# Sparse attention and a feed-forward layer on one core: key, query and output transposes of the later batches moved from TensorE to DMA

## The chip, the core and the metric

The kernel runs on one core of a Trainium2 chip. The core has five engines that run side by side, each through its own instructions in order: TensorE (PE; its weight loads are listed apart as PEld), VectorE (DVE), ScalarE (ACT), GpSimd (POOL) and SyncE (SP). Transfers run on 16 DMA engines and are issued from the queues of GpSimd and SP. The metric is the device time of one execution in microseconds; lower is better. The time before is 329.82 us, the median of three runs (329.7 to 330.48).

## The reference

Inputs q, k, v have 8 batches, 8 heads, 576 tokens and 64 columns, in float32. The first four heads attend to a band of 32 tokens, the last four to every 32nd token, and the result, laid side by side as 4608 tokens by 512 columns, goes through a feed-forward layer with 2048 hidden columns:

```python
scores = scale * np.matmul(q, k.transpose(0, 1, 3, 2))
rel = pos[:, None] - pos[None, :]
mask_local = (rel >= 0) & (rel < 32)
mask_strided = (rel >= 0) & (pos[None, :] % 32 == pos[:, None] % 32)
...                                     # heads 0-3 band, heads 4-7 strided
attn = softmax(np.where(mask, scores, -1e9))
x = np.matmul(attn, v)                  # then (batch, token) x (head, column)
h = x @ w_in
r = np.maximum(h, 0.0)
out = (s * (r * r) + b) @ w_out
```

## The kernel before

**Layouts.** Attention runs by batch `b` (0 to 7) and by pair of heads `m` (0 to 3). Pairs 0 and 1 are band heads ("loc", names ending in `l`), pairs 2 and 3 strided heads ("str", names ending in `s`); `mm` is the pair's number within its kind. For band pairs the 576 tokens lie as 6 pieces of 96; for strided pairs as 8 pieces of 72, each holding the tokens of one residue modulo 8. Scores need queries and keys with the 64 columns on the partitions, so both must be transposed, two heads at a time (128 rows). `qD_loc` and `qD_str` hold the queries of one pair, `kT_loc` its band keys, `kTs` its strided keys. The output of a pair, `x_nat`, has tokens on the partitions and must be transposed once more into `xT[m]`, which the feed-forward layer reads as its moving operand.

**Who transposes.** TensorE does most of it: line 357 for queries and keys (six matmuls against the identity for a band pair, eight for a strided one) and line 529 for outputs. Each result lies in PSUM and is copied out by ACT or DVE (line 286). Band queries and keys first go through a pairing copy (`qp`, `kp`, posted by `pair_post`), which lays two heads side by side. Two kinds go by DMA transpose from SP already: the strided keys from b = 3 on (`k_dma`, line 399) and the band outputs from b = 2 on (`x_dma`, line 551).

**The rest of attention.** Line 429 is the scores, line 443 the exponential on ACT, line 451 the mask on DVE, line 481 the product with v (AV), lines 496 and 507 the division on DVE.

**Feed-forward.** Nine tiles `T` of 512 tokens. Line 574 is the first product (64 matmuls of 512 columns for a tile), line 592 the ReLU on ACT, line 598 the square on DVE, line 609 the second product (again 64), line 620 the eviction on DVE and line 624 the store. A tile needs `xT` of all four pairs for the one or two batches that its tokens belong to.

**What sets the order.** No hardware decides it. A planner written in the kernel, `Plan`, walks through an estimated time and writes one fixed list of instructions for each engine. A `Step` is one TensorE instruction with its estimated ns, the keys it needs and those it makes; `plan.post` places work on the cheapest of the engines it may run on ("A", "V", "P", "D" for ACT, DVE, GpSimd and DMA by SP), when its needs are met in estimated time. A DMA posted as "D" counts 1000 ns and then 5000 ns of latency. Loads get an estimated arrival from `landing(cost)`. In the main loop an attention step is taken while attention is behind `due()`, which grows with the feed-forward steps done, and otherwise a feed-forward step; attention steps come from a window of four pairs. Once the lists stand, an engine waits at each instruction for its real inputs, and nothing behind that instruction can pass it.

**Loads.** `fetch_qk(b)` and `fetch_v(b)` issue a batch's loads from GpSimd, converting float32 to float16 on the way. `ql`, `kl`, `qs` have two buffers each; `ks` are two fixed tiles. From b = 3 on, a fetch is preceded by two tiny copies on GpSimd (line 664), which wait until the strided keys of the batch before have been transposed. The band keys `kl` have 96 partitions, each holding six consecutive tokens of each head (1536 bytes of float32 in one piece). The last load of a batch is its v.

Of the kernel before, what the change touches and what calls it, by code (L numbers as in the profile page):

```python
# [9 lines left out]
FP16 = mybir.dt.float16  # L10
# [100 lines left out]
def kernel(  # L111
# [11 lines left out]
    nc = tc.nc  # L123
    B, H, S, D = q.shape
# [11 lines left out]
    LQ, LT, LPAD = 96, 6, 32  # L136
    SQ, ST = 72, 8
# [16 lines left out]
    inp = ctx.enter_context(tc.tile_pool(name="inp", bufs=2))  # L154
# [26 lines left out]
    kT_loc = [const.tile([128, LPAD + S], FP16, name=f"kT_loc{i}") for i in range(2)]  # L181

    qD_loc = [const.tile([128, LT, 2, LQ], FP16, name=f"qD_loc{i}") for i in range(2)]
    qD_str = [const.tile([128, ST, 2, SQ], FP16, name=f"qD_str{i}") for i in range(2)]
    xT = [const.tile([128, NTOK], FP16, name=f"xT{i}") for i in range(4)]

    SR = 80
    ks = [const.tile([SR, 4 * ST * D], FP16, name=f"ks{i}") for i in range(2)]

    sched = ctx.enter_context(tc.manual_schedule())  # L190
    plan = Plan()

# [3 lines left out]
    NL, NS = 4 * LT * D, 4 * ST * D  # L196
# [3 lines left out]
    def view_l(src, b):  # L200
        return src[b, 0:4].rearrange("h (p j) d -> p h (j d)", j=LT)
# [11 lines left out]
    def h4(ap):  # L213
        return ap.rearrange("p (h x) -> p h x", h=4)
# [21 lines left out]
    loaded = {}  # L236
    paired = {}

    def load_qk(b):
        for name, src in (("q", q), ("k", k)):  # L240
            tl = inp.tile([LQ, NL], FP16, tag=name + "l", name=name + "l")
            nc.gpsimd.dma_start(out=h4(tl), in_=view_l(src, b))
            loaded[b, name + "l"] = tl
        for name, src in (("q", q), ("k", k)):
            ts = inp.tile([SQ, NS], FP16, tag="qs", name="qs") if name == "q" else ks[b % 2]
            if name == "k" and b in (2, 3):
                nc.gpsimd.memset(ts[64:SR], 0.0)
            load_s(ts, src, b)
            loaded[b, name + "s"] = ts

    def load_s(dst, src, b):
        for r in (slice(0, 64), slice(64, SQ)) if b < 2 else (slice(0, SQ),):
            nc.gpsimd.dma_start(out=h4(dst)[r], in_=view_s(src, b)[r])
# [31 lines left out]
    def copy_on(eng, **kw):  # L285
        {"A": nc.scalar.copy, "V": nc.vector.tensor_copy, "P": nc.gpsimd.tensor_copy}[eng](**kw)  # L286

    def pair_post(b, name, mm, key):

        if (b, name) not in paired:  # L290
            paired[b, name] = None

        def g(eng):
            if paired[b, name] is None:
                paired[b, name] = inp.tile([LQ, 2, LT, 2 * D], FP16, tag=name + "p",
                                           name=name + "p")
            from_ = loaded[b, name + "l"]
            copy_on(eng, out=paired[b, name][:, mm].rearrange("p j (e d) -> p e j d", e=2),
                    in_=from_.rearrange("p (m e j d) -> p m e j d", m=2, e=2, d=D)[:, mm])
        plan.post([key], {"A": 810, "V": 350, **({"P": 750.0} if b == 0 else {})}, g,  # L300
                  [("in", name + "l", b, mm)])
# [37 lines left out]
    def pair_steps(b, m):  # L339

        loc = m < 2
        nq, nt = (LQ, LT) if loc else (SQ, ST)
        sfx = "l" if loc else "s"
        mm = m % 2
        nk = 128 if loc else SQ
        st = {}
        steps = []
        id_ = (b, m)
# [43 lines left out]
                    s.posts = [([key], {"A": 640, "V": 757 if loc else 453}, g, [("k", id_), group])]  # L392
            return s

        k_by_dma, x_by_dma = b >= 3, b >= 2

        def k_dma(eng):
            st["k"] = qkp.tile([128, ST, SR], FP16, tag="kTs", name="kTs")
            nc.sync.dma_start_transpose(out=st["k"], in_=ks[b % 2][:, 1024 * mm:1024 * mm + 1024])
            loaded[b, "kTs", mm] = st["k"]  # L400

        if k_by_dma and not loc:

            plan.post([("in", "ks", b, mm), ("s", (b - 1, m), 2)], {"D": 1000.0}, k_dma,
                      [("k", id_)])
        for name in ("q", "k"):
            if k_by_dma and not loc and name == "k":
                continue
            gr = group_of("t", b, m, True)
            for j in range(nt):  # L410
                steps.append(trans(name, j, gr))
        last_t = steps[-1]

        per_s = 2 if loc else 3

# [55 lines left out]
        per = nt if loc else nt // 2  # L471
# [53 lines left out]
        def xtrans(j, group):  # L525
# [21 lines left out]
                s.posts = [([key], {"A": 640, "V": 455 if loc else 756}, g, [("xT", b, m), group])]  # L547
            return s

        def x_dma(eng):  # L550
            nc.sync.dma_start_transpose(
                out=xT[m][:, b * S:(b + 1) * S].rearrange("d (t p) -> d t p", t=nt),
                in_=st["x"].rearrange("p t d -> p (t d)"))

        if x_by_dma and loc:
            plan.post([("x", id_, e, nt - 1) for e in range(2)], {"D": 1000.0}, x_dma,
                      [("xT", b, m)])
        else:
            gr = group_of("t", b, m)
            for j in range(nt):  # L560
                steps.append(xtrans(j, gr))
        return steps, st["last_av"], last_t


    gts = {}
# [77 lines left out]
    def arrive(keys, at):  # L643
        for k in keys:
            plan.done[k] = at
# [4 lines left out]
    def landing(cost):  # L650

        nonlocal ring
        ring = max(ring, plan.t + 2000.0) + cost

        return ring + (6000.0 if plan.t > 60000.0 else 0.0)

    def both(name, b):
        return [("in", name, b, mm) for mm in range(2)]

    def fetch_qk(b):  # L660
        for mm in range(2):
            if (b - 1, "kTs", mm) in loaded:

                nc.gpsimd.tensor_copy(out=gate[0:1, 2 + mm:3 + mm],
                                      in_=loaded[b - 1, "kTs", mm][0:1, 0, 0:1])
        load_qk(b)
        for name in ("q", "k"):
            plan.done["raw", name, b] = landing(1700)
            for mm in range(2):
                pair_post(b, name, mm, ("raw", name, b))  # L670
        for name in ("qs", "ks"):
            arrive(both(name, b), landing(2000))

    def fetch_v(b):
        load_vl(b)
        arrive(both("vl", b), landing(5000))
        if b < LONG_V:
            early_v(b)
        else:
            load_vs(b)  # L680
            arrive(both("vs", b), landing(5000))
# [70 lines left out]
    def when_all(what, b, fn):  # L752

        def g():
            left[what, b] = left.get((what, b), 4) - 1
            if left[what, b] == 0:
                fn()
        return g

    for b in range(B):  # L760
        for m in range(4):
            steps, last_av, last_t = pair_steps(b, m)
            att.append(steps)
            if b + 2 < B:

                last_t.after = when_all("t", b, lambda b=b: plan.post(
                    [("fetch_v", b + 1) if b else ("free",)] +
                    [("k", (bk, mk)) for bk in (b, b + 1 if b > 1 else b) for mk in range(2, 4)],
                    {"P": 0.0},
                    lambda eng: fetch_qk(b + 2), [("fetch", b + 2)]))  # L770
                last_av.after = when_all("av", b, lambda b=b: plan.post(
                    [("fetch", b + 2)] + both("vs", b), {"P": 0.0}, lambda eng: fetch_v(b + 2),
                    [("fetch_v", b + 2)]))
# [55 lines left out]
    while i2 < len(f2) or any(at_i[p] < len(att[p]) for p in range(len(att))):  # L829
# [21 lines left out]
        for o in order:  # L851
            s = f1[i1] if o == 1 else f2[i2]
# [4 lines left out]
        if cand is not None and (att_done < due() or main is None):  # L857
            s = att[cand][at_i[cand]]
# [45 lines left out]
```

The softmax here doesn't subtract the row's maximum and nothing guards it: scores larger than these inputs give would overflow.

## Time and profile before

| | before |
|---|---|
| time, median of 3 | 329.82 us |
| span of the profiled execution | 328.6 us |
| HBM read and written | 38.15 MB, 9.44 MB |
| packets of the GpSimd queue | 50032, 18.65 MB |
| packets of the SP queue | 23114, 13.74 MB |
| PE first product, line 574 | 576 matmuls, of which 432 read the later weight tiles |
| PE second product, line 609 | 576 matmuls |
| PE transposes, lines 357 and 529 | 368 and 152 |
| DMA transposes of xT and kTs | 12 and 10 |

The page gives busy time by engine, then groups of instructions by line, engine and tile. A matmul's duration there overlaps the next one's, so durations of TensorE don't add up to time; distances between starts do. The kernel has three stretches: up to about 40 us inputs and weights arrive and the first attention batch runs; up to about 231 us attention and feed-forward matmuls are mixed; after that only the feed-forward layer is left. The same stretches can be seen in the busy tenths of the 40 slices of the span:

```profile
PE   8898899999999999999999999999999999999995
DVE  5566946698877768676878777586442423332311
ACT  2775943598958856647555556543432433243100
POOL 6482548640931820551065000000000000000000
DMA  7999999999994995599369940131001000101021
```

Each digit is a tenth of the busy share of a slice of 8.2 us. TensorE is full from the sixth slice on, GpSimd, which only issues loads and helps a little at first, ends at about 187 us with the last batch's loads, and the DMA engines show gaps from about 107 us on.

### The profile page before, as it was taken

The page shows a single profiled execution, that of the slowest core. Times are in us where ns is not written, and L with a number is a line of the kernel's source. Part 1 is how long each engine was busy: PE and PEld are TensorE (multiplying, and loading weights), DVE is VectorE, ACT ScalarE, POOL GpSimd, SP SyncE. Part 2 cuts the span into 40 slices and gives each one's busy share as a digit, 9 for nine tenths or more (in the row PEclk, how much of TensorE's full clock was granted, in tenths as well). Part 3 has the DMA queues.
Part 4 walks back from the last instruction along what each step waited for, and adds up shares of the span by engine and source line. Part 5 has one row for each costly group of instructions (what it writes and reads, how often), then busy time and mean ns, then how long its engine had stood idle before and what let it go on. Part 6 is the DMA issues. An engine that isn't in the chain of part 4 may idle for free.

```text
span 328.6 us, 6386 instructions
## 1 busy us (share of the span) xinstructions
PE 318.7 (97%) x2424; PEld 181.7 (55%) x2424; DVE 201.2 (61%) x552; ACT 171.6 (52%) x322; POOL 84.8 (26%) x123
## 2 busy tenths in 40 slices
PE   8898899999999999999999999999999999999995
PEld 3673655666556656556655655555544544444442
DVE  5566946698877768676878777586442423332311
ACT  2775943598958856647555556543432433243100
POOL 6482548640931820551065000000000000000000
PEclk9999999999999999999999999999999999999998
DMA  7999999999994995599369940131001000101021
GB/s 115 184 153 206 214 164 166 219 179 93 141 137 92 163 98 73 66 193 121 72 98 160 81 118 2 50 53 64 2 32 62 36 32 33 64 15 51 32 98 64
DMA packets 73176, 32.80 MB, mean 100 GB/s; under 512 B 54586, under 2 KB 67514, under 8 KB 73146
## 3 DMA queue, kind: packets, MB, share of 16 engines
q0 software_dynamic: 50032, 18.65, 61.1%
q1 hardware_dynamic: 23114, 13.74, 18.3%
q8 instruction: 19, 0.31, 0.4%
q14 instruction: 11, 0.09, 0.1%
HBM read 38.15 MB, written 9.44 MB: 145 GB/s over the span
## 4 chain that ended last, share of the span: by engine, by line
PE 85%; DMA 7%; ACT 4%; POOL 2%; issue 1%; DVE 0%; SPq 0%; POOLq 0%
PE ps_f L609 37%; PE ps_f L574 34%; DMA ql<-in_q_dram 5%; PE ps_s L429 4%; PE ps_a L481 4%; PE ps_t L357 3%; DMA w_out_sb<-in_v_dram 2%; PE ps_t L529 1%; PE ps_a L632 1%; ACT pt L443 1%; ACT qD_str L286 1%; ACT qD_loc L286 1%; POOL w_in L273 1%; POOL v_loc L286 1%; ACT xT L286 0%
## 5 line engine op out<-in xcount | busy, mean ns | idle before, releaser
L609 PE MATMUL ps_f<-w_out_sb,gT 128*128 128x512 f16 x576 | 151.6, 379 | 0.3 <-DVE gT L598 0.3
L592 ACT ACTIVATE u<-ps_f 128x512 f16<-128x512 f32 x136 | 80.6, 596 | 81.7 <-PE ps_f L574 61.1
L574 PE MATMUL ps_f<-xT,w_in_sb 128*128 128x512 f16 x432 | 118.3, 379 | 1.3 <-DMA w_in_sb<-in_moe_w_in_dram 1.3
L598 DVE TENSOR_TENSOR gT<-u 128x512 f16<-128x512 f16 x144 | 59.7, 419 | 54.2 <-ACT u L592 53.0
L609 PEld LDWEIGHTS <-gT 128*128 128x128 f16 x576 | 54.3, 98 | 49.5 <-DVE gT L598 0.6
L574 PEld LDWEIGHTS <-w_in_sb 128*128 128x128 f16 x432 | 46.5, 114 | 33.3 <-DMA w_in_sb<-in_moe_w_in_dram 2.0
L443 ACT ACTIVATE pt<-ps_s 128x384 f16<-128x384 f32 (+2 forms) x96 | 44.6, 488 | 17.0 <-PE ps_s L429 16.2
L481 PEld LDWEIGHTS <-pt 72*72 72x72 f16 (+1 forms) x448 | 36.9, 119 | 13.9 <-DVE pt L451 0.2
L620 DVE SCALAR_TENSOR_TENSOR o<-ps_f,s_sb,bcs 128x512 f32<-128x512 f32 x36 | 26.8, 746 | 19.7 <-PE ps_f L609 19.5
L574 PE MATMUL ps_f<-xT,w_in 128*128 128x512 f16 x136 | 36.0, 380 | 0.1
L507 DVE TENSOR_TENSOR x_nat<-ps_a,rec 72x256 f16<-72x256 f32 (+1 forms) x76 | 35.0, 461 | 1.6
L260 POOL DMA_DIRECT2D v_loc<-in_v_dram x28 | 24.3, 893 | 1.2 <-issue 0.6
L496 DVE RECIPROCAL rec<-ps_a 72x4 f32<-72x4 f32 (+1 forms) x76 | 13.7, 180 | 17.9 <-PE ps_a L481 15.3
L481 PE MATMUL ps_a<-v_str,pt 72*72 72x65 f16 x204 | 22.8, 196 | 0.0
L574 PEld LDWEIGHTS <-w_in 128*128 128x128 f16 x144 | 15.1, 113 | 9.6
L429 PE MATMUL ps_s<-qD_str,kTs 128*72 128x144 f16 x128 | 18.8, 226 | 0.2 <-ACT kTs L286 0.2
L429 PE MATMUL ps_s<-qD_loc,kT_loc 128*128 128x192 f16 x96 | 17.3, 246 | 0.7 <-ACT pt L443 0.3
L265 POOL DMA_DIRECT2D v_str<-in_v_dram x16 | 13.6, 849 | 13.7 <-PE ps_f L574 2.7
L481 PE MATMUL ps_a<-v_loc,pt 128*96 128x65 f16 x150 | 17.1, 203 | 0.0
L451 DVE TENSOR_TENSOR pt<-pt,mask_loc 128x384 f16<-128x384 f16 x42 | 14.4, 351 | 3.9 <-ACT pt L443 3.6
L451 DVE TENSOR_TENSOR pt<-pt,mask_str 72x432 f16<-72x432 f16 (+1 forms) x42 | 14.1, 348 | 3.6 <-ACT pt L443 3.3
L429 PEld LDWEIGHTS <-kTs 128*72 128x72 f16 x128 | 12.7, 113 | 5.4 <-issue 0.7
(91 smaller groups left out, 283.6 us busy)
## 6 DMA issues: line engine op xcount, KB each, us to landing
out_dram<-o SPq DMA_DIRECT2D x36, 256.0 KB, 2.0
ql<-in_q_dram POOLq DMA_DIRECT2D x8, 288.0 KB, 5.2
kl<-in_k_dram POOLq DMA_DIRECT2D x8, 288.0 KB, 6.5
v_loc<-in_v_dram POOLq DMA_DIRECT2D x28, 80.0 KB, 9.3
w_out_sb<-in_moe_w_out_dram POOLq DMA_DIRECT2D x4, 512.0 KB, 12.0
qs<-in_q_dram POOLq DMA_DIRECT2D x6, 288.0 KB, 8.0
ks<-in_k_dram POOLq DMA_DIRECT2D x6, 288.0 KB, 9.2
v_str<-in_v_dram POOLq DMA_DIRECT2D x16, 72.0 KB, 7.0
```

Source lines behind the costliest of these rows:

```text
L260: nc.gpsimd.dma_start(out=vl[:, h, 1:LT, 0:D], in_=rest[:, h])
L429: nc.tensor.matmul(out=st["s", g][0:nk, c:c + 2 * nq], lhsT=(st["k"][:, i * nq:i * nq + nk] if loc else st["k"][:, i, 0:SQ]), rhs=st["q"][ ...
L443: nc.scalar.activation(out=pt[0:nk, 0:2 * n].rearrange("k t c -> k (t c)"), in_=st["s", g][0:nk, 0:2 * n * nq], func=AF.Exp, scale=scale)
L451: nc.vector.tensor_tensor(out=pt[0:nk, 0:2 * n], in0=pt[0:nk, 0:2 * n], in1=mask, op=ALU.mult)
L481: nc.tensor.matmul(out=st["a"][0:nq, j % per, :], lhsT=st["pt", g][0:nk, i, :], rhs=vt[0:nk, 2 * mm + e, j, :])
L496: nc.vector.reciprocal(out=st["rec", e, j][0:nq, 0:per], in_=st["pa", e, j][0:nq, 0:per, D:D + 1])
L507: nc.vector.tensor_tensor(out=st["x"][:, j0:j0 + per, 64 * e:64 * e + 64], in0=st["pa", e, j][0:nq, 0:per, 0:D], in1=st["rec", e, j][0:nq, ...
L574: nc.tensor.matmul(out=gts["h", T, ft], lhsT=(w_in_sb[min(ft // 4, 2) - 1][:, ct, :] if ft > 3 else w_in0[ct]).rearrange("p (c x l) -> p c ...
L592: nc.scalar.activation(out=gts["u", T, ft], in_=gts["h", T, ft], func=AF.Relu)
L598: nc.vector.tensor_tensor(out=gts[T][:, ft, :], in0=u, in1=u, op=ALU.mult)
L609: nc.tensor.matmul(out=gts["o", T, ts], lhsT=gts[T][:, ft, ts * 128:(ts + 1) * 128], rhs=w_out_sb[:, ft, :], start=(ft == 0), stop=(ft == ...
L620: nc.vector.scalar_tensor_tensor(out=o, in0=gts["o", T, ts], scalar=s_sb[:, 0:1], in1=bcs, op0=ALU.mult, op1=ALU.add)
```

## The change

From b = 3 on, three more kinds of transpose leave TensorE. The band keys are loaded in another layout (token 96 t + p on partition p), so that no pairing copy is needed, and `kT_loc` is written by a DMA transpose straight from `kl`. The strided queries are transposed by DMA into a tile `qTs` in SBUF, and a copy (`q_spread`) spreads that over `qD_str`. The strided outputs can't be put into token order by the transpose itself, so `x_out` stores them to a buffer in DRAM in token order and `x_in` transposes them from there into `xT`. TensorE keeps the band queries, the scores and AV, and all transposes of the first three batches. [...] `qs` becomes a tile of 80 rows whose last 16 are cleared once. The fetch of batch b + 2 is now posted once per batch, with the queries and keys of batch b among its needs. The purpose is to take work from TensorE.

```diff
+    KB_DMA, QS_DMA, XS_DMA = 3, 3, 3
+    x_dram = [tc.dram_tile([S, 128], FP16, name=f"x_dram{i}") for i in range(4)]
...
+            if name == "k" and b >= KB_DMA:
+                dst = tl.rearrange("p (m t e d) -> p m e t d", m=2, t=LT, e=2)
+                for h in range(4):
+                    nc.gpsimd.dma_start(out=dst[:, h // 2, h % 2],
+                                        in_=src[b, h].rearrange("(t p) d -> p t d", p=LQ))
+            else:
+                nc.gpsimd.dma_start(out=h4(tl), in_=view_l(src, b))
...
-        k_by_dma, x_by_dma = b >= 3, b >= 2
+        k_by_dma = b >= (KB_DMA if loc else 3)
+        q_by_dma = b >= QS_DMA and not loc
+        x_by_dma = b >= (2 if loc else XS_DMA)
         def k_dma(eng):
+            if loc:
+                st["k"] = kT_loc[mm]
+                nc.sync.dma_start_transpose(
+                    out=st["k"][:, LPAD:LPAD + S].rearrange("d (t p) -> d t p", t=nt),
+                    in_=loaded[b, "kl"][:, 768 * mm:768 * mm + 768])
+                return
...
+        def q_dma(eng):
+            st["qT"] = inp.tile([128, ST, SR], FP16, tag="kp", name="qTs")
+            nc.sync.dma_start_transpose(out=st["qT"],
+                                        in_=loaded[b, "qs"][:, 1024 * mm:1024 * mm + 1024])
+        def q_spread(eng):
+            st["q"] = qD_str[mm]
+            for e in range(2):
+                hs = slice(64 * e, 64 * e + 64)
+                copy_on(eng, out=st["q"][hs, :, e, :], in_=st["qT"][hs, :, 0:SQ])
...
+            plan.post([("in", "qs", b, mm), ("s", (b - 1, m), 2)], {"D": 1000.0}, q_dma,
+                      [("qT", id_)])
+            plan.post([("qT", id_)], {"P": 2000.0, "V": 560.0, "A": 1300.0}, q_spread,
+                      [("q", id_)])
...
+        def x_out(eng):
+            nc.sync.dma_start(out=x_dram[2 * (b % 2) + mm].rearrange("(p j) d -> p j d", j=nt),
+                              in_=st["x"])
+        def x_in(eng):
+            nc.sync.dma_start_transpose(out=xT[m][:, b * S:(b + 1) * S],
+                                        in_=x_dram[2 * (b % 2) + mm])
...
+            plan.post([("x", id_, e, j) for e in range(2) for j in (per - 1, nt - 1)],
+                      {"D": 1000.0}, x_out, [("xd", id_)])
+            plan.post([("xd", id_)], {"D": 1000.0}, x_in, [("xT", b, m)])
...
+            if name == "k" and b >= KB_DMA:
+                arrive(both("kl", b), landing(4600))
+                continue
...
-                last_t.after = when_all("t", b, lambda b=b: plan.post(
-                    [("fetch_v", b + 1) if b else ("free",)] +
-                    [("k", (bk, mk)) for bk in (b, b + 1 if b > 1 else b) for mk in range(2, 4)],
-                    {"P": 0.0},
-                    lambda eng: fetch_qk(b + 2), [("fetch", b + 2)]))
+                if m == 0:
+                    plan.post(
+                        [("fetch_v", b + 1) if b else ("free",)] +
+                        [("q", (b, mk)) for mk in range(4)] + [("k", (b, mk)) for mk in range(4)] +
+                        [("k", (b + 1 if b > 1 else b, mk)) for mk in range(2, 4)],
+                        {"P": 0.0}, lambda eng, b=b: fetch_qk(b + 2), [("fetch", b + 2)])
```

More of the change, by code (lines that the diff above doesn't have):

```diff
@@ L241, in load_qk @@
             tl = inp.tile([LQ, NL], FP16, tag=name + "l", name=name + "l")
-            nc.gpsimd.dma_start(out=h4(tl), in_=view_l(src, b))
             loaded[b, name + "l"] = tl
-        for name, src in (("q", q), ("k", k)):
-            ts = inp.tile([SQ, NS], FP16, tag="qs", name="qs") if name == "q" else ks[b % 2]
-            if name == "k" and b in (2, 3):
+            if name == "k" and b >= KB_DMA:
[5 more added lines that the diff above has]
+                nc.gpsimd.dma_start(out=h4(tl), in_=view_l(src, b))
+        for name, src in (("q", q), ("k", k)):
+            if name == "k":
+                ts = ks[b % 2]
+            elif b < QS_DMA + 2:
+                ts = inp.tile([SR, NS], FP16, tag="qs", name="qs")
+            else:
+                ts = loaded[b - 2, "qs"]
+            if name == "k" and b in (2, 3) or name == "q" and b in (QS_DMA, QS_DMA + 1):
                 nc.gpsimd.memset(ts[64:SR], 0.0)
@@ L294, in g @@
             if paired[b, name] is None:
-                paired[b, name] = inp.tile([LQ, 2, LT, 2 * D], FP16, tag=name + "p",
-                                           name=name + "p")
+                paired[b, name] = inp.tile([128, 2, LT, 2 * D], FP16, tag=name + "p",
+                                           name=name + "p")[0:LQ]
             from_ = loaded[b, name + "l"]
@@ L400, in k_dma @@
             loaded[b, "kTs", mm] = st["k"]
-        if k_by_dma and not loc:
-            plan.post([("in", "ks", b, mm), ("s", (b - 1, m), 2)], {"D": 1000.0}, k_dma,
-                      [("k", id_)])
+        def q_dma(eng):
[7 more added lines that the diff above has]
+                copy_on(eng, out=st["q"][hs, :, e, :], in_=st["qT"][hs, :, 0:SQ])
+        if k_by_dma:
+            plan.post([("in", "k" + sfx, b, mm), ("s", (b - 1, m), 2)], {"D": 1000.0}, k_dma,
+                      [("k", id_)])
+        if q_by_dma:
+            plan.post([("in", "qs", b, mm), ("s", (b - 1, m), 2)], {"D": 1000.0}, q_dma,
+                      [("qT", id_)])
+            plan.post([("qT", id_)], {"P": 2000.0, "V": 560.0, "A": 1300.0}, q_spread,
+                      [("q", id_)])
         for name in ("q", "k"):
-            if k_by_dma and not loc and name == "k":
+            if (k_by_dma if name == "k" else q_by_dma):
                 continue
@@ L411, in pair_steps @@
                 steps.append(trans(name, j, gr))
-        last_t = steps[-1]
         per_s = 2 if loc else 3
@@ L557, in pair_steps @@
                       [("xT", b, m)])
+        elif x_by_dma:
+            plan.post([("x", id_, e, j) for e in range(2) for j in (per - 1, nt - 1)],
+                      {"D": 1000.0}, x_out, [("xd", id_)])
+            plan.post([("xd", id_)], {"D": 1000.0}, x_in, [("xT", b, m)])
         else:
@@ L561, in pair_steps @@
                 steps.append(xtrans(j, gr))
-        return steps, st["last_av"], last_t
+        return steps, st["last_av"]
     gts = {}
@@ L761 @@
         for m in range(4):
-            steps, last_av, last_t = pair_steps(b, m)
+            steps, last_av = pair_steps(b, m)
             att.append(steps)
             if b + 2 < B:
-                last_t.after = when_all("t", b, lambda b=b: plan.post(
-                    [("fetch_v", b + 1) if b else ("free",)] +
-                    [("k", (bk, mk)) for bk in (b, b + 1 if b > 1 else b) for mk in range(2, 4)],
-                    {"P": 0.0},
-                    lambda eng: fetch_qk(b + 2), [("fetch", b + 2)]))
+                if m == 0:
[4 more added lines that the diff above has]
+                        {"P": 0.0}, lambda eng, b=b: fetch_qk(b + 2), [("fetch", b + 2)])
                 last_av.after = when_all("av", b, lambda b=b: plan.post(
```

## The prediction

> **What bounds the kernel now.** I read the busy times first, then the chain that ended last, then TensorE's timeline, and only then the waits and the transfers.
>
> ```profile
> PE 318.7 (97%) x2424; PEld 181.7 (55%) x2424; DVE 201.2 (61%) x552; ACT 171.6 (52%) x322; POOL 84.8 (26%) x123
> ...
> PE 85%; DMA 7%; ACT 4%; POOL 2%; issue 1%; DVE 0%; SPq 0%; POOLq 0%
> ```
>
> The first line is the busy row of the page, the second the chain by engine. PE is busy 97% of the span and is 85% of the chain; the DMA and ACT shares lie in the start-up, before about 40 us. PE overlaps its matmuls, so the busy share does not say what one instruction costs. The timeline does, by the distance from one start to the next (columns: start, busy, engine, line, operation, tiles, count):
>
> ```profile
> 208.18 0.29 PE L357 MATMUL ps_t<-ident,kp 96*128 96x96 f16 x3
> 208.31 0.38 PE L574 MATMUL ps_f<-xT,w_in_sb 128*128 128x512 f16 x1
> ...
> 230.70 0.29 PE L529 MATMUL ps_t<-ident,x_nat 72*128 72x72 f16 x4
> 230.83 1.03 PE L574 MATMUL ps_f<-xT,w_in 128*128 128x512 f16 x4
> 231.70 0.30 PE L529 MATMUL ps_t<-ident,x_nat 72*128 72x72 f16 x4
> ```
>
> Three band-key transposes move the next start by 0.13 us (43 ns each), four strided transposes by 0.13 us (33 ns each), four 512-column matmuls by 0.87 us (216 ns each). From 72 us to the last matmul at 324.4 us, those spacings times the instruction counts leave only 1.2 us over, nearly all at 89.9-91.3 us. So after 72 us the time is the sum of TensorE's spacings: what leaves TensorE leaves the end, and every new wait of TensorE is added to it.
>
> The next views are a line of the waits (total, times, longest), and the landings of one transpose:
>
> ```profile
> POOL gate L664 <- DMA kTs<-ks: 52.0, 8, 11.5
> ```
>
> ```profile
> L551 SPq DMA_TRANSPOSE xT<-x_nat x12: 1197/1217/1302, 70.4 to 217.4; - x12
> ...
> DMA to landing us min/median/max: 2.5/2.6/7.7
> ```
>
> Last, busy time by stage (PE, PE loads, DVE, ACT, POOL, then clock, DMA share, GB/s):
>
> ```profile
> 57.00:81.00 24.00, 23.76 (x245) 15.24 (x244) 18.98 (x60) 18.69 (x36) 9.63 (x12) 1.00 1.36 166
> 81.00:105.00 24.00, 23.64 (x219) 14.62 (x218) 19.69 (x61) 18.00 (x36) 11.13 (x15) 1.00 1.49 128
> 105.00:135.00 30.00, 30.00 (x253) 18.06 (x252) 22.02 (x65) 20.44 (x40) 10.55 (x15) 1.00 1.28 106
> ```
>
> GpSimd waits 52 us in eight waits for the strided keys' transposes before it fetches: loads have slack. A DMA transpose holds SP for 1.2 us and lands in 2.6 us, but the one issued at 70.4 us, among loads, took 7.7. DVE and ACT have 20-30% to spare per stage.
>
> **What the skill says.** "TensorE: Matmul & The Clock Gate", Part 4: PE-mode transpose, gives about 275 ns for a transpose inside a kernel; at that price 220 would be 60 us. This trace has 196-206 ns of duration and 33-43 ns of spacing; the measurement decides. "DMA: Bandwidth & Descriptors", Specifications, puts full rate at pieces of 512 B or more; the packet records agree: 128 B take 32 ns, 768 B 79 ns. The same page, Issuing engines are not separate DMA queues, says that all queues share 16 engines; the 2.5 against 7.7 us above agrees. The same page, Two DMAs through the same engine are not ordered, has a reader of DMA-written bytes wait for the first DMA's semaphore; hence the wait between the two halves of the trip through DRAM. The trace of before has no such pair.
>
> **The change, part by part** (batches count from b = 0; it acts on b = 3 to 7).
>
> TensorE loses 10 band-key pairs x 6 = 60 at 43 ns = 2.6 us, 10 strided-query pairs x 8 = 80 at 33-35 ns = 2.7 us, 10 strided-output pairs x 8 = 80 at 33 ns = 2.6 us. Sum **7.9 us, all on the path**; nothing is added there. With no new wait: 329.8 - 7.9 = 321.9.
>
> ACT and DVE lose 10 band-key evictions, 10 output evictions (the xT copy from PSUM is 0.64 us on ACT) and the key pairing copies (kp, 0.35 us on DVE). The query evictions become copies from SBUF of the same size (6 pairs on DVE, 3 on ACT, 1 on GpSimd). Worth nothing: both engines were off the path.
>
> The planner paces attention by TensorE time, so cheaper batches come sooner: by the order of instructions the last AV matmul is followed by 502 of the 1152 feed-forward matmuls instead of 434, and a batch of attention takes some 26 us instead of 30. Costs nothing while loads keep up.
>
> DMA per batch. The new band keys arrive as 2304 packets of 128 B instead of 384 of 768 B: (2304 x 32 - 384 x 79) ns / 16 engines = +2.7 us. Six more transposes of 576-640 packets at 18 ns: 0.7 us each, +4.1 us; two writes of 72 packets of 2 KB at 84 ns: +0.8 us. Batch 5's loads ran from 105.7 to 123.4 us, 17.7 us; with these, 17.7 + 2.7 + 4.9 = 25.3 us against a batch of 26. It fits, barely.
>
> New waits. The order is static, so a late transfer stops the engine whose next instruction needs it. (a) Band keys: one SP transpose per pair, then TensorE's scores, with all feed-forward matmuls behind them. For b = 3 the loads of start-up still run; before, they landed until 77.8 us, now +2.7 = 80.5. The key transpose is issued at about 71.8 (after the one at 70.4) and, like that one, gets through only as the loads end: about 81.2. By order and spacings the first such score comes at 80.1 us: **1.1 us**, between 0 (landing in 2.6) and 3 (both pairs late). (b) Queries: the copy to qD waits for the transpose, and exps, masks and ReLU copies queue behind it on ACT or DVE, then TensorE behind their PSUM banks. On GpSimd the fetch queues behind it, which has slack. (c) Outputs: store plus transpose. From the nearest rows 2.0 + 2.6 = 4.6 us free, and 6.3 (a store at 55.1 us) + 7.7 = 14.0 under loads; the planner allows 12 (D, 1000 + 5000 ns, twice). By the order, the tiles that start near 132 and 154 us get just these 12 us, the later ones 20 and more. For (b) and (c) together I take **1.0 us**, the middle of 0 (free values) to 2 (14.0 - 12 once). (d) SP issues some 10 transposes a batch, 12 us of 26; output stores behind a waiting transpose have three buffers: nothing.
>
> Sum: 329.8 - 7.9 + 1.1 + 1.0 = **324.0**.
>
> **The rivals.** *All hidden*: every transfer lands within its allowance, 321.9; for it, the 52 us of slack; against it, the 7.7 us landing. *Late pieces*: two pairs late in (a), and queries and both tiles of (c) late, 3 + 3 = 6 us: 328. *The loads become the loop* (the other side): each fetch waits for the previous batch's key transpose, which waits for its keys. If transposes amid loads take 7.7 us and then set the next fetch free, a turn is 17.7 + 2.7 + 7.7 + 2.7 (second transpose) = 30.8 us, 4.8 over the batch, 19 us over four turns. Before, band keys landed at 111.4 for use near 132, 20 us of slack; the first fetch moves some 6 us later and attention 4-6 sooner, leaving 8: 321.9 + 19 - 8 = 333. For it: DMA shares of 1.3-1.5 in these stages; against it: packets overlap, and after the loads the trace moves a transpose in 1 us.
>
> **Chances.** Forecast 0.5, all hidden 0.2, late pieces 0.15, loop 0.15. Leaving out the loop, and a bit below the hidden case, gives 321.3 to 329.0. Faster by over 0.3% (under 328.8): the first two and two thirds of the third, 0.8; within 0.3% 0.07; slower 0.13.
>
> **What would show it.** The changed profile should have 2204 matmuls, the strided transposes gone after b = 2, the last AV near 208 us, and unchanged spacings. Step (a) shows as PE waiting for kT_loc near 80 us; (b) as ACT or DVE waiting for qTs; (c) as PE or PEld waiting for xT. Hidden: no such waits. Loop: PE idle in every batch to 210 us, and GpSimd's wait for kTs gone. I am wrong if a transpose from DRAM takes much more than one from SBUF, or if SP's queue holds keys behind a late output.

## The result and the profile after

The changed kernel takes **339.18 us** (median of six runs, 337.36 to 339.79) against 329.79 us before (six runs): the ratio is 1.0264, 95% interval 1.0228 to 1.0299. It became slower, by 9.4 us, where 5.8 us less were forecast. All ratios below compare with the kernel before on the same chip and leave out runs that are more than 1.5% above the fastest of their kernel, while medians are of all runs, so that the two can differ.

The page of the changed kernel, busy time and then the chain:

```profile
PE 316.5 (94%) x2204; PEld 175.9 (52%) x2204; DVE 190.7 (57%) x536; ACT 161.5 (48%) x306; POOL 102.7 (30%) x142
...
PE 67%; DMA 20%; DVE 4%; ACT 3%; POOL 2%; issue 1%; SPq 1%; POOLq 0%; ACTq 0%
```

TensorE has the 2204 matmuls that were expected. But its share of the chain fell from 85% to 67%, and that of DMA rose from 7% to 20%: the end now waits for transfers. The landings of the transposes show which (the strided queries first, then the strided keys):

```profile
L429 SPq DMA_TRANSPOSE qTs<-qs x10: 1267/1969/2589, 73.7 to 195.4; - x10
...
DMA to landing us min/median/max: 4.6/8.1/10.9
```

```profile
L424 SPq DMA_TRANSPOSE kTs<-ks x10: 1202/1302/3000, 75.3 to 200.9; - x10
...
DMA to landing us min/median/max: 4.1/5.7/8.9
```

The trace tells the landing of only four of the ten of each kind, so these medians are rough. Before, the transposes of the strided keys landed in a median of 2.7 us and those of the band outputs in 2.6. Now the strided keys take 5.7 us and the band outputs 8.4, and the queries, which are new, take 8.1. The planner's order allows a transfer 6. The busy time by stage shows what that does to TensorE (PE, PE loads, DVE, ACT, POOL, clock, DMA share, GB/s):

```profile
81.00:105.00 24.00, 22.86 (x189) 13.54 (x188) 19.29 (x56) 15.42 (x29) 16.55 (x20) 1.00 1.20 110
105.00:135.00 30.00, 27.34 (x198) 15.64 (x197) 20.14 (x60) 14.41 (x28) 13.27 (x18) 0.94 1.54 143
135.00:166.00 31.00, 27.39 (x204) 15.93 (x203) 19.93 (x64) 17.48 (x34) 12.87 (x18) 1.00 1.46 149
166.00:196.00 30.00, 28.78 (x223) 16.82 (x221) 21.50 (x67) 16.93 (x32) 12.79 (x18) 1.00 1.44 150
196.00:226.00 30.00, 25.65 (x170) 14.21 (x171) 17.23 (x53) 12.96 (x26) 0.00 (x0) 0.89 0.96 102
```

The same stages before, of which the prediction shows the first two:

```profile
135.00:166.00 31.00, 31.00 (x263) 18.45 (x262) 23.41 (x65) 18.69 (x35) 10.58 (x15) 1.00 1.19 115
166.00:196.00 30.00, 30.00 (x251) 17.68 (x250) 24.03 (x64) 16.04 (x31) 10.33 (x14) 1.00 1.16 119
196.00:226.00 30.00, 30.00 (x251) 17.79 (x249) 21.38 (x60) 17.40 (x33) 0.00 (x0) 1.00 0.17 38
```

Before, TensorE was full in all of these stages but for 0.4 us in the first. Now it idles in each, and in two of them its clock is lower as well. To size the gaps, I take the distance from one matmul start to the next after 70 us, less the usual distance for such a pair. Gaps over 0.3 us come to 14.7 us, before to 0.5 us. By what ended them, the 14.7 us are 7.2 us for `kT_loc`, 4.0 us for an output `x_nat` of DVE, 2.8 us for `xT` from DRAM and 0.8 us for `kTs` (this one by the wait of its weight load). Two of them in TensorE's timeline:

```profile
138.43 0.59 PE L627 MATMUL ps_f<-xT,w_in 128*128 128x512 f16 x2 [1.14 <-DMA xT<-x_dram]
...
140.55 0.50 PE L469 MATMUL ps_s<-qD_loc,kT_loc 128*128 128x192 f16 x4 [1.18 <-DMA kT_loc<-kl]
```

The brackets give the idle time and what ended it: first a strided output that came through DRAM (stored by `x_out`, transposed by `x_in`) for the start of a feed-forward tile, then the band keys of b = 5. TensorE can't pass either.

The sum of the change: the last matmul starts at 333.3 us, 8.9 us later than before. The moved transposes give -7.9, the gaps +14.2. The matmuls of 512 columns that run at half speed after a long gap give +2.5 (below). The start-up was 1.4 us shorter in this execution, and the remaining 1.5 us lie in shorter gaps and in slow small matmuls.

### The profile page after: what moved, and what is told of

Read it like the earlier page. It is cut to its first block, busy times and chain, and to the rows that moved or that the text cites. A ratio compares the mean times of both kernels' runs of the same rounds, so it can differ in the third digit from the quotient of the medians.

```text
span 337.5 us, 6004 instructions
## 1 busy us (share of the span) xinstructions
PE 316.5 (94%) x2204; PEld 175.9 (52%) x2204; DVE 190.7 (57%) x536; ACT 161.5 (48%) x306; POOL 102.7 (30%) x142
## 4 chain that ended last, share of the span: by engine, by line
PE 67%; DMA 20%; DVE 4%; ACT 3%; POOL 2%; issue 1%; SPq 1%; POOLq 0%; ACTq 0%
PE ps_f L662 31%; PE ps_f L627 27%; DMA kT_loc<-kl 5%; DMA ql<-in_q_dram 5%; DMA qTs<-qs 3%; PE ps_s L469 3%; PE ps_a L521 3%; DMA xT<-x_dram 2%; DMA x_dram<-x_nat 2%; DMA w_out_sb<-in_v_dram 2%; DMA kTs<-ks 2%; PE ps_t L374 1%; DVE v_str L303 1%; PE ps_a L685 1%; ACT pt L483 1%
## 5 line engine op out<-in xcount | busy, mean ns | idle before, releaser
L662 PE MATMUL ps_f<-w_out_sb,gT 128*128 128x512 f16 x576 | 148.5, 382 | 0.0
L627 PE MATMUL ps_f<-xT,w_in_sb 128*128 128x512 f16 x432 | 115.7, 382 | 0.3 <-DMA w_in_sb<-in_moe_w_in_dram 0.3
L483 ACT ACTIVATE pt<-ps_s 128x384 f16<-128x384 f32 (+2 forms) x96 | 43.5, 489 | 20.0 <-PE ps_s L469 19.0
L521 PEld LDWEIGHTS <-pt 72*72 72x72 f16 (+1 forms) x448 | 31.4, 121 | 19.9 <-issue 4.4
L536 DVE RECIPROCAL rec<-ps_a 72x4 f32<-72x4 f32 (+1 forms) x76 | 13.7, 180 | 26.0 <-PE ps_a L521 25.7
L469 PE MATMUL ps_s<-qD_loc,kT_loc 128*128 128x192 f16 x96 | 15.7, 254 | 6.7 <-DMA kT_loc<-kl 6.1
L303 ACT COPY qD_loc<-ps_t 64x576 f16<-64x576 f16 x24 | 15.2, 632 | 8.1 <-PE ps_t L374 7.8
L521 PE MATMUL ps_a<-v_str,pt 72*72 72x65 f16 x204 | 15.4, 198 | 3.7 <-DVE x_nat L547 3.7
L469 PE MATMUL ps_s<-qD_str,kTs 128*72 128x144 f16 x128 | 16.0, 233 | 0.9 <-ACT u L645 0.6
L717 POOL COPY gate<-kTs 1x1 f16<-1x1 f16 x8 | 3.7, 460 | 40.8 <-DMA kTs<-ks 40.7
L469 PEld LDWEIGHTS <-kT_loc 128*128 128x128 f16 x96 | 8.6, 100 | 13.7 <-DMA kT_loc<-kl 7.7
```

The source lines that it names most:

```text
L469: nc.tensor.matmul(out=st["s", g][0:nk, c:c + 2 * nq], lhsT=(st["k"][:, i * nq:i * nq + nk] if loc else st["k"][:, i, 0:SQ]), rhs=st["q"][ ...
L483: nc.scalar.activation(out=pt[0:nk, 0:2 * n].rearrange("k t c -> k (t c)"), in_=st["s", g][0:nk, 0:2 * n * nq], func=AF.Exp, scale=scale)
L521: nc.tensor.matmul(out=st["a"][0:nq, j % per, :], lhsT=st["pt", g][0:nk, i, :], rhs=vt[0:nk, 2 * mm + e, j, :])
L627: nc.tensor.matmul(out=gts["h", T, ft], lhsT=(w_in_sb[min(ft // 4, 2) - 1][:, ct, :] if ft > 3 else w_in0[ct]).rearrange("p (c x l) -> p c ...
L662: nc.tensor.matmul(out=gts["o", T, ts], lhsT=gts[T][:, ft, ts * 128:(ts + 1) * 128], rhs=w_out_sb[:, ft, :], start=(ft == 0), stop=(ft == ...
```

## The experiments

The three constants of the diff move one kind of transpose each, so the parts can be had alone. All are set to 99 in the first kernel, one of them to 3 in the next three:

```diff
-    KB_DMA, QS_DMA, XS_DMA = 3, 3, 3
+    KB_DMA, QS_DMA, XS_DMA = 99, 99, 99
```

| kernel | moved | median us | ratio to before | 95% interval |
|---|---|---|---|---|
| e1 | none | 329.34 | 0.9997 | 0.9984 to 1.0009 |
| e2 | band keys | 327.45 | 0.9935 | 0.9913 to 0.9957 |
| e3 | strided queries | 333.94 | 1.0144 | 1.0124 to 1.0164 |
| e4 | strided outputs | 326.96 | 0.9927 | 0.9911 to 0.9943 |
| e5 | keys and outputs | 332.07 | 1.0060 | 1.0040 to 1.0081 |

**e1, nothing moved.**

> The new code with all three kinds left on TensorE (only the new post of the fetch, once per batch with the queries and keys of the batch among its needs, and the 80-row query tile remain). Theory A (the late transposes cost the time): as before, 329.8 us within 1 us. Rival (the later fetch costs it): the fetches start later here too, and the time goes to 333 us or more.

The same as before: the new code by itself costs nothing that these runs can tell. It does not test a later fetch, since the fetches of e1 start only 0.5 us later than before (82.5 instead of 82.0 us for b = 4, 167.6 instead of 167.1 for b = 7), while the changed kernel's start at 85.6 and 177.3.

**e2, keys alone.**

> Only the band keys go by DMA (60 TensorE transposes, 2.6 us less; loads in 128-byte packets, 2.7 us longer per batch). Theory A (each transpose that shares the DMA engines with the loads lands late by itself): PE still waits for kT_loc, 4 to 7 us in all, and the time is 331 to 334 us. Rival B (SP's queue, which is in order, is the cause: a transpose stands behind others that wait): with only two more transposes a batch the queue is free, and the time is 327 to 328 us.

0.65% or 2.1 us off, near the 2.6 us that leave TensorE; no gap over 0.3 us is left after 70 us. Both theories had parts right: rival B's time came in, but the key transposes do land late all the same, and nobody minds (the trace tells two of the ten landings):

```profile
L419 SPq DMA_TRANSPOSE kT_loc<-kl x10: 1196/1208/1475, 71.2 to 176.3; - x10
...
DMA to landing us min/median/max: 6.2/7.3/8.5
```

Here a late landing did no harm, as the consumer stood later still.

**e3, queries alone.**

> Only the strided queries go by DMA (80 TensorE transposes, 2.7 us less). Theory A: the transposes are issued while the batch's loads still run, DVE or ACT waits for qTs, 2 to 4 us, plus slow TensorE after it; 329 to 332 us. Rival B: 327 to 328 us.

1.4% slower, more than theory A had. Nearly all of it is one wait of TensorE, 4.0 us, and the half speed that follows it, 2.6 us more. DVE's timeline, then TensorE's:

```profile
84.13 0.41 DVE L651 TENSOR_TENSOR gT<-u 128x512 f16<-128x512 f16 x1
89.71 0.92 DVE L303 COPY qD_str<-qTs 64x576 f16<-64x576 f16 x2 [5.16 <-DMA qTs<-qs]
90.66 0.36 DVE L491 TENSOR_TENSOR pt<-pt,mask_loc 128x384 f16<-128x384 f16 x1
90.93 0.42 DVE L651 TENSOR_TENSOR gT<-u 128x512 f16<-128x512 f16 x1
```

```profile
87.23 0.38 PE L662 MATMUL ps_f<-w_out_sb,gT 128*128 128x512 f16 x1
91.41 0.61 PE L662 MATMUL ps_f<-w_out_sb,gT 128*128 128x512 f16 x1 [3.80 <-DVE gT L651]
```

The second query transpose of b = 3 is issued at 81.1 us, just as the loads of b = 4 start (80-81 us), and lands 8.6 us later. DVE's copy of it stands ahead of a mask and a `gT` that TensorE needs, so a query nobody was in a hurry for stops the feed-forward layer.

**e4, outputs alone.**

> Only the strided outputs go through DRAM (80 TensorE transposes, 2.6 us less). Theory A: no consumer is nearer than the tile start, the waits for xT from DRAM are 0 to 2 us, 327 to 329 us. Rival B (SP waits at the second half of the trip for the first, and that holds the strided keys behind it): the strided keys' transposes and with them the fetches come later, and PE waits for kTs; 329 to 332 us.

0.7% or 2.5 us off, for 2.6 us of TensorE work: hidden, as theory A had it. The one gap over 0.3 us in its trace is the one at 89-91 us that the kernel before has too.

**e5, keys and outputs together.**

> Band keys and strided outputs by DMA, strided queries on TensorE. Each alone took 2.0 and 2.5 us off. Theory (the query transposes are what brings the waits; keys and outputs fit): the gains add, 324.5 to 325.5 us, no wait of PE for kT_loc. Rival (any two kinds overfill the DMA engines beside the loads): PE waits for kT_loc from the batch b = 5 on, 327 us or more.

My theory fell, and the rival's 327 us or more came in, though its waits for `kT_loc` start with b = 6, at 159 us. The parts that gain 2.1 and 2.5 us alone lose 0.6% together, and the waits for the band keys are there without any query transpose. The two lines of its waits (total, times, longest):

```profile
PEld L469 <- DMA kT_loc<-kl: 5.8, 2, 4.2
PE ps_s L469 <- DMA kT_loc<-kl: 4.9, 2, 3.7
```

So it is no single kind. The next runs ask what makes them late together.

**e7, half of the later loads left out.** The changed kernel, its order kept, without v for b = 5 to 7:

```diff
     def fetch_v(b):
+        if b >= 5:
+            for n in ("vl", "vs"):
+                arrive(both(n, b), landing(5000))
+            return
         load_vl(b)
```

> The changed kernel in its own order, but v of the batches b = 5 to 7 isn't loaded (AV reads the v of an earlier batch): about half of those batches' load packets are gone, nothing else moves. Theory (the transposes land late because they share the DMA engines with the loads): transposes in these batches land in 3 to 5 us, the waits after 135 us (some 9 us with their slow TensorE) mostly go, 328 to 332 us. Rival (SP's queue order holds them back): the waits stay, 337 to 339 us.

323.18 us, ratio 0.9823 (0.9779 to 0.9867), below what even the theory had. The same stages as above, in its profile (of the slowest of its four runs, 326.33 us):

```profile
105.00:135.00 30.00, 27.23 (x197) 15.61 (x196) 19.98 (x61) 14.39 (x28) 5.72 (x9) 0.94 1.10 141
135.00:166.00 31.00, 31.00 (x236) 18.38 (x235) 22.91 (x74) 19.93 (x39) 5.61 (x9) 1.00 1.01 144
166.00:196.00 30.00, 30.00 (x236) 17.92 (x235) 22.40 (x71) 19.37 (x38) 6.61 (x9) 1.00 1.06 159
196.00:226.00 30.00, 30.00 (x189) 16.01 (x188) 17.08 (x49) 11.40 (x22) 0.00 (x0) 1.00 0.25 70
```

Up to 135 us it is the changed kernel, idle included. From there on TensorE is full, with every transpose still on DMA and SP's order the same. The queries of b = 5 to 7 whose landing the trace tells take 2.7 to 3.1 us (three of six); in the changed kernel three of them took 4.6 to 10.9. So the later waits come from the loads. All twenty traces agree. Of the transposes from SBUF to SBUF whose landing they tell, 166 had no packet of a load start within 2.5 us of their issue, and landed in a median of 2.7 us (2.5 to 5.0); 86 had more than 300 such packets, and took a median of 8.0 us (3.0 to 11.8). That both run on the same 16 DMA engines, as the prediction has it, fits this; what the runs themselves show is that the loads make the transposes late.

**e9, larger pieces for the band keys.** Four transfers as in the changed kernel, each with rows of 768 bytes in SBUF instead of six pieces of 128:

```diff
-                    nc.gpsimd.dma_start(out=dst[:, h // 2, h % 2],
-                                        in_=src[b, h].rearrange("(t p) d -> p t d", p=LQ))
+                    nc.gpsimd.dma_start(out=tl[:, 384 * h:384 * h + 384],
+                                        in_=src[b, h].rearrange("(p j) d -> p (j d)", j=LT))
```

> The changed kernel in its own order, but the band keys of b = 3 to 7 arrive in pieces of 768 bytes instead of 128, still by four transfers (the keys then lie in another order than their queries' mask expects, nothing else changes). 2.7 us of DMA work a batch less. Theory (DMA engines shared by loads and transposes, each us of load work counts): part of the 14 us of idle TensorE goes, 332 to 337 us. Rival (only the number of transposes counts): as the changed kernel, 337 to 339.5 us.

333.18 us, 1.0102 (1.0027 to 1.0177): six of the 9.4 us are gone (four runs, 331.6 to 335.4), and the gaps of TensorE are 8.3 instead of 14.7 us, with the number of transposes unchanged. The rival falls. So the small pieces of the new key layout, which saves the pairing copy, account for most of the loss against the kernel before.

**e6, more room in the order.**

```diff
-    LAT = {"A": 70.0, "V": 70.0, "P": 70.0, "D": 5000.0}
+    LAT = {"A": 70.0, "V": 70.0, "P": 70.0, "D": 9000.0}
```

> All three kinds by DMA, with the planner's latency of a DMA at 9000 instead of 5000 ns: the order leaves each transpose 10 us instead of 6. Theory (the consumers stand too near in a static order): most of the 14 us of idle TensorE goes, 322 to 327 us. Rival (the loads' loop is longer than a batch, so that lateness only moves): PE idles at other places, 333 us or more.

328.14 us, 0.9913 (0.9881 to 0.9945). The twenty runs spread from 323.3 to 330.8 us and the ratio rests on the ten lowest; by the medians it is 0.9954. The gaps fall to 5.3 us, of which 3.8 are one wait for `xT` from DRAM. This is the theory's side of the question, one microsecond above its range in the median: room cures most of the lateness and does not merely move it.

**e8, queries from b = 4.**

> Queries by DMA only from b = 4, keys and outputs from b = 3. Theory (each batch's queries bring their own wait): the first wait, at about 112 us, stays or moves by a batch, and the later waits for kT_loc stay: 336 us or more. Rival (the first query batch meets the loads of the start and that delay is carried through all later batches by the fetches that wait for the keys): 326 to 330 us.

334.63 us, 1.0159 (1.0122 to 1.0196), between the two. Without the queries of b = 3 the gaps still come to 11.9 us, from 132 us on.

**e10 to e12, larger pieces for v.** With LONG_V = 8 the strided v of all batches comes in pieces of 1024 bytes.

```diff
-    LONG_V = 4
+    LONG_V = 8
```

> The changed kernel with LONG_V = 8: the strided v arrives in pieces of 1024 bytes for every batch and is spread by DVE or ACT (4 more copies of 0.27 us a batch), 2.8 us of DMA work a batch less and one transfer instead of four on GpSimd; the order of instructions changes with it. Theory: 331 to 336 us. Rival: 337 us or more, or slower through DVE.

This one stays unclear: 20 runs spread from 326.4 to 341.3 us (median 333.76; the ratio, 0.9984, 0.9952 to 1.0016, rests on the seven lowest). Perhaps its order is just at the edge, and small shifts of landings decide; that is not shown. As the order changes with LONG_V, too, these three runs don't tell its effect from that of the lighter loads; e9, which keeps the order, does.

> LONG_V = 8 and the planner's DMA latency at 9000 ns. Theory (both causes, shared DMA engines and consumers that stand too near): below the 328.1 us of the 9000 ns alone, 322 to 326 us. Rival (the two repair the same waits): 327 to 329 us.

**324.00 us, ratio 0.9823 (0.9755 to 0.9890)**: this is the version that beats both kernels, by 5.3 us the one before (329.27 us on the same chip) and by 15 us the changed one, and in the theory's range: with the room given, the larger pieces bring some 4 us more (328.1 to 324.0). Its page again in two lines:

```profile
PE 310.5 (97%) x2204; PEld 174.2 (54%) x2204; DVE 193.2 (60%) x552; ACT 160.9 (50%) x306; POOL 91.1 (28%) x130
...
PE 83%; DMA 7%; DVE 3%; ACT 3%; POOL 2%; issue 1%; SPq 0%; POOLq 0%
```

The DMA share of the chain is back at 7%. The gaps are 2.3 us.

> Keys and outputs by DMA, queries on TensorE, LONG_V = 8. Without the larger pieces it ran in 332.1 us with 6.2 us of waits, all after 155 us. Theory: 2.8 us of load work a batch less brings the waits below 2 us, 324 to 327 us. Rival: the waits stay, 330 us or more.

326.30 us, 0.9860 (0.9778 to 0.9942), gaps 2.1 us instead of 6.2: the theory, within its range of time and just above the 2 us of waits.

**e13, e14 and e16, controls.**

> Control: no kind moved, LONG_V = 8. Before, TensorE had 0.5 us of idle after 70 us, so lighter loads can bring nothing there: 329 to 330.5 us. Rival (the larger v pieces are what sped up the combined version): 324 to 327 us.

> Control: no kind moved, LONG_V = 8 and 9000 ns of DMA latency in the planner. Theory: 329 to 331 us, as TensorE's work is unchanged. Rival (the other order is worth something by itself): 327 us or less.

> Keys and outputs moved, queries on TensorE, LONG_V = 8, 9000 ns. TensorE has 2.7 us more work than with all three. Theory (with room, TensorE's work decides): 325 to 327 us, slower than the 324.0 us of all three. Rival (fewer transposes, fewer waits): below 324 us.

e13: 328.83 us, 0.9985 (0.9977 to 0.9992). e14: 329.11 us, 0.9996 (0.9979 to 1.0012). So the two remedies by themselves bring 0.15% (0.23% at the end of the interval); the gain of e11 is that of the moved transposes. e16: 325.25 us, 0.9874 (0.9858 to 0.9890), slower by 1.3 us in the median than e11, about half of the 2.7 us that the queries are on TensorE. Its interval and that of e11 overlap, so the last step isn't settled.

**e15, e17 and e18, the queries again.**

> Only the queries moved, with 9000 ns in the planner. At 5000 ns one transpose that landed 8.6 us after its issue held DVE for 5.2 us and TensorE for 4.0. Theory (the order left it 6 us): with 10 us of room the wait is gone, 326.5 to 328 us. Rival (any later consumer meets the next fetch's loads as well): 330 us or more.

335.08 us, 1.0148 (1.0105 to 1.0191): room alone doesn't cure the queries; DVE waits for `qTs` three times, for 2.3 us at most. In its trace the second query transpose of b = 6 and of b = 7 is issued just as the copy of the first ends (165.8 and 195.3 us), so I suspected their buffers: `qTs` shares two buffers with the pairing copies `kp`. The last two kernels have the same order on TensorE and differ in the buffers alone:

```diff
-            st["qT"] = inp.tile([128, ST, SR], FP16, tag="kp", name="qTs")
+            st["qT"] = inp.tile([128, ST, SR], FP16, tag="vs", name="qTs")
...
```

> Only the queries moved, from b = 4 on (64 transposes, 2.2 us less), qTs in the two buffers of the pairing copies kp. Theory (the second query transpose waits for the first one's copy, and DVE then waits for it): DVE waits for qTs 1 to 5 us in all, 329 to 333 us. Rival (the loss came from b = 3 and the loads of the start): 327 to 328 us.

> The same, with qTs in the buffers of the staged strided v, which nobody uses after b = 3. Theory: the second transpose follows the first by 1.3 us, the waits for qTs go, 327 to 328 us. Rival (the waits come from sharing the DMA engines with loads): as e17.

327.16 us (0.9930, 0.9903 to 0.9958) and 326.72 us (0.9914, 0.9887 to 0.9942). My theory fell again: neither trace has a wait for `qTs`, and the shared buffers cost nothing that these runs can tell. Nor did the second transpose follow the first by 1.3 us with buffers of its own: for b = 4 it was issued at 101.8 us in e18 and at 102.5 in e17, as SP had other transposes to issue first. From b = 4 on, at the planner's own latency, the queries alone are hidden. What made e3 slow is b = 3, whose second query transpose met the loads of b = 4: the wait and the slow stretch after it, 6.6 us, are most of the 7.2 us between e3 and e18. Why e15 has later waits of its own, in another order and with shared buffers, isn't settled.

## Why the prediction was wrong

**What bounds the kernel, and the size of the saving: right.** After 72 us the time is the sum of TensorE's spacings. e2, e4 and e18 give 2.1, 2.5 and 2.6 us for transposes priced at 2.6, 2.6 and 2.2 us, and e11, with nearly all waits gone, has its last matmul at 317.1 us, 7.3 us earlier than before. The order was as foreseen too: 502 feed-forward matmuls stand behind the last AV, which the waits put at 225.2 us instead of the forecast 208.

**The new waits: wrong, and this is the step that failed.** The prediction added 1.1 us for (a), the band keys, and 1.0 us for (b) and (c), queries and outputs. Measured were 7.2 us for (a), 2.7 us for (b), where DVE's copy waited for the queries before an output, 2.8 us for (c), and 0.8 us for the strided keys, which had no term at all. The other 1.3 us after DVE come from a memset (last section). Three things were behind it.

- The 7.7 us landing was taken for an exception of the start-up. It was the usual case for a transpose amid loads. In the kernel before, the fetch of a batch followed the key transposes, so they seldom met, and the median of 2.6 us was that of transposes without loads beside them. The new kinds have no such order: a median of 8.1 us for the queries and 7.3 for the outputs from DRAM, and even the old kinds were drawn in. e7 shows it by taking loads away. The prediction would call itself wrong if a transpose from DRAM took much more than one from SBUF; the only one in all the traces that met no load packet, in e11, landed in 2.6 us, which speaks for the loads here too.
- (a) was worked out for b = 3, where the gap for `kT_loc` was in fact nil, and not for b = 5 to 7, where all 7.2 us lie. There the prediction saw only slack from the landing of the keys (20 us, in its rival of the loop). For b = 7, with 4.3 of the 7.2 us, the keys landed at 187.2 us and their transposes were issued at 187.4 and 188.8, but TensorE waited for them until 198.5 and 201.7, while loads ran until 210.1. For b = 5 the transpose was not even issued when its input landed, since SP takes its list in order, behind outputs and stores that wait for DVE: the keys had landed by 123.9 us and their first transpose was issued at 132.5 us, beside loads that ran until 138.6.
- (d) priced SP's queue at nothing, from its 12 us of issue in 26, and left out its waits, as for b = 5. By themselves they cost nothing, though: in e7 the same transpose is issued at 132.6 us and TensorE has no gap there. Another order of SP's list was not tried.

**DMA per batch: nearly right in the sum, wrong in the conclusion.** The loads of b = 5, 6 and 7 took 22.2, 25.7 and 32.8 us from first issue to last landing, against 25.3 with transposes in the estimate; only b = 7 went far beyond it. "It fits, barely" should have been read as: loads are nearly always in flight when a transpose is issued. e9 shows what the 2.7 us of small key pieces alone were worth: 6 us.

**The rival on the other side** had 333 us and a turn of 30.8 us. The fetches did start every 30 to 31 us (85.6, 116.4, 146.6, 177.3), but after the first turn they did so before as well (82.0, 105.7, 135.7, 167.1). Of its two marks, TensorE idle in every batch to 210 us is there; the other, GpSimd's wait for `kTs` gone, is not:

```profile
POOL gate L717 <- DMA kTs<-ks: 40.7, 6, 14.4
```

GpSimd still waits 41 us for the strided keys, so the loads are not a loop that runs without pause. The rival had the contention right and the loop wrong, and it too was 6 us short.

**TensorE's clock had no term.** After some long gaps TensorE takes the 512-column matmuls at half speed. In the changed kernel's timeline, after a gap of 2.5 us, and then the stage as above (the clock is the third number from the end):

```profile
114.68 0.39 PE L521 MATMUL ps_a<-v_str,pt 72*72 72x65 f16 x4 [2.53 <-DVE x_nat L547]
115.21 0.94 PE L469 MATMUL ps_s<-qD_str,kTs 128*72 128x144 f16 x6
115.94 1.49 PE L627 MATMUL ps_f<-xT,w_in_sb 128*128 128x512 f16 x3
117.22 0.45 PE L469 MATMUL ps_s<-qD_str,kTs 128*72 128x144 f16 x2
```

```profile
114.50:117.90 3.40, 3.08 (x17) 1.88 (x17) 2.75 (x10) 1.74 (x4) 2.33 (x5) 0.50 0.44 95
```

Three matmuls from 115.94 to 117.22 us are 427 ns each, where they are 216 at full speed, and the granted clock of this stretch is 0.50. So a long wait can be paid for once as a gap and again after it: 2.5 us of such matmuls in the whole execution, from this stretch and one of 6.8 us that began at 199.8. The Trainium skill's page "TensorE: Matmul & The Clock Gate", Why this matters for your kernels, warns of gaps over about 3 us; here 2.5 us were enough, though not in every trace (last section).

**The confidence: wrong.** The range, 321.3 to 329.0, was built on the waits' free values at one end and on "late pieces" of 6 us at the other, and the true sum of gaps was nearly 15. The chance of getting slower was put at 0.13.

## What to carry to other kernels

When work moves from a full engine to a shared one, price the waits with the latency that the shared engine has when it is busy, and take it from where the new work will stand: an old median tells of the old neighbours. In a static order, look for each transfer at the instruction that consumes it and at what stands behind that on its engine, and at what stands ahead of the transfer in its queue; then give the order the room (here 10 us instead of 6) and the shared engines less to do (here larger pieces). Parts that are each free alone can still collide together, so add their demands and not their times.

## What the runs showed of the hardware that I had not expected

Half speed after a gap: in all these traces, after 70 us, there are 12 places where one matmul starts 2.6 us or more after the one before. In eight of them the clock falls to 0.5 during the gap or at most 1.4 us after it, and stays there for 3.4 or 6.8 us by the trace's record. It does so twice more, in e5 and e9, at shorter gaps, of 1.2 and 1.6 us of idle time, and does not at one of 2.9 us in e10. So the length of one gap does not decide alone; what else does isn't shown.

A memset on GpSimd can hold up a copy on DVE. The change added two memsets that clear the last rows of `qs`. In the changed kernel's timeline, DVE and then GpSimd:

```profile
88.22 3.03 DVE L303 COPY v_str<-vs 72x512 f16<-72x512 f16 x4
91.17 0.40 DVE L547 TENSOR_TENSOR x_nat<-ps_a,rec 72x256 f16<-72x256 f32 x1
```

```profile
89.28 1.82 POOL L264 MEMSET qs<- 16x2048 f16 x1
```

The last of the four copies runs from 89.28 to 91.25 us, over all of the memset; the median of such a copy is 0.29 us in e2. The output `x_nat` behind it ended TensorE's gap of 1.1 us at 90-92 us. The Trainium skill's page "GPSIMD Engine Reference", in its table of specifications, says that GpSimd shares its SBUF interfaces with VectorE; the trace agrees, with a factor of about seven for this copy. The traces of e7, e9, e10, e11, e17 and e18 show the same: a copy from SBUF to SBUF that starts during such a memset ends 0.15 us after it, in all seven. The page's row also names DVE instructions with two SBUF inputs; here those keep their time beside a memset, in e9 for instance two multiplications `gT` of 0.43 and 0.42 us between 86.6 and 87.9. No run tried this by itself.
